# Query blocks in the order 0, 1, 3, 2: attention's projections added to totals on chip in a fused attention and product-key-expert kernel

## The chip, the cores and the metric

The kernel runs on one core of one Trainium2 chip. The metric is the device time of one execution in microseconds; the figure of a kernel is the median of its runs. The engines are called here as in the profile: PE is TensorE (matrix products), PEld its weight loads, DVE is VectorE, ACT is ScalarE, POOL is GpSimd, and SP is SyncE, which here only issues DMA transfers.

## The reference

The input is x of 2048 tokens by 512 numbers, float32. It is normalised (xn), and two parts are added to it: attention with 32 heads that share one key head and one value head of 16 numbers, and a layer of 4096 experts of which each token picks two per head by product keys.

```python
xn = _layernorm(x)
# part A: attention, one K and V head for 32 query heads
q = (xn @ wq).reshape(B, S, 32, 16).transpose(0, 2, 1, 3); k = xn @ wk; v = xn @ wv
p = softmax(einsum("bhqd,bkd->bhqk", q, k) * 16 ** -0.5)
A = einsum("bhqk,bkd->bhqd", p, v).transpose(0, 2, 1, 3).reshape(B, S, 512) @ wo
# part B: experts, 32 heads, 64 x 64 keys, two experts a head
s1, s2 = scores of the two halves of xn @ w_q against k1 and k2       # 64 each
two best of s1 and of s2 -> four candidates -> the two best (top_e), g = softmax(top_s)
act = gelu(einsum("nd,nhkd->nhk", xn, u[top_e]))
B = einsum("nhk,nhk,nhkd->nd", g, act, v[top_e])
return x + A + B
```

## The kernel before

The 2048 tokens are 16 tiles of 128 tokens, in four blocks of four tiles: block 0 is tiles 0 to 3, block 3 tiles 12 to 15. Everything is computed in one program whose instruction order is written out by hand.

**Attention.** A unit is four heads of one query block (`units`, L293); there are 32, in the order of the blocks, eight units a block. A unit goes over 16 chunks of 128 keys. For each chunk `scores` (L314) makes two score tiles on PE (L318) and their exponentials on ACT (L321), and `pv` (L324) multiplies by the values on PE (L332). Two units are a pair; `unit_tail`, `pair_load`, `pair_invert`, `pair_spread` and `pair_tail` bring the sums of the exponentials to memory and back, invert them, and write the normalised result of the pair to a tile `on`. Four pairs make a query block. Its four tiles are then multiplied by `wo`: `block_out(qb, j)` (L423) is one projection, eight matmuls of 128 x 512 into one PSUM tile (tag `x`, three buffers, which all other products share).

**Experts, by gather.** For blocks 0 and 1 each chosen expert's rows of u and v are gathered by GpSimd (L883) into one of twelve buffers (tag `g`, `NGB`), DVE takes the dot product with xn (L895), and adds the weighted row to the token's total `ACC[t]` (L930). The total starts as x, in a tile `xa` that holds total and xn of a tile of tokens. Block 1 takes over the four `xa` tiles of block 0 when that is done (`load_phase2_tile`, L988).

**Experts, dense.** For blocks 2 and 3 all 4096 experts are computed as matrix products (`dense`, L648). First a table of gates is formed by one-hot products (L752), written to memory (`d_g`, L760) and read back by blocks of experts (`fetch_gates`, L669). `first_gates` (L731) reads the first two gate blocks and loads x into the totals (`da`) of the block of tokens. Then 32 blocks of expert weights follow: `fetch` loads block b (`rw`, two buffers), `split` rounds it on ACT (L687) and takes the rest on DVE (L688), L799 multiplies by xn, ACT and DVE form the weighted activations (L821 to L835), and `sums` (L773) multiplies by v (L783) and adds to the totals (L786). The rounding of weight block b + 2 is put on the list for ACT when the product of weight block b starts (b even) or has ended (b odd).

**The order.** The outer loop runs over d; one pass is one call of `att_steps` (L1040) with i = 2d, called a step in this document: two chunks of one unit. Within a step stand, in this order: stores left by the step before (`run(STORES)`), scores of the first chunk, the products with the values of the step before, `mid()` (ACT's and DVE's lists: the copies `ON_ACT`, the dots, the expert sums, and interleaved with them the list `BEHIND`), scores of the second chunk, a projection if one is due, and `fill()`. `fill` runs the generator of the experts' scores and dense products (`run_scores`) until a count of planned work, `spent`, has reached the step's aim, which grows by (948 - 17) / 256 units a step, but by no more than 4 units in a step. A projection is booked with 3.6 units. `yield None` in the generator ends a step's fill. Two of the twelve gather buffers are lent (`lent`) to `wo` at the end of each query block.

**Where the two parts meet.** The attention part of a block and the expert part of the same block are ready at different times. `fin` is one small buffer of 128 x 512 in the pool `late`. For a projection whose experts' part isn't done (blocks 0 and 1), ACT copies the projection to `fin` (L440), and it goes to memory (`d_part`, L441); when the experts are done `experts_out` loads it into `fin` (L420), DVE adds the total (L452), and the sum is stored to `out`. For block 2 it is the other way round: the dense total goes to `d_part` first (L459), and at each projection `load_fin` brings it back, DVE adds the projection (L433), and the sum is stored. Block 3's projection and its dense total end together: `last_out_a` and `last_out_b` add the projection to `ACC[12 + j]` on chip (L411). A block's projections are due at (i - 144) % 128 = 0, 4, 8 and 12: one in every second step, in steps 144 to 156, 272 to 284 and 400 to 412.

SP issues its transfers strictly in the order of the program; one that must wait for a buffer or for data holds all that follow.

Of the kernel before, what the change touches and what calls it, by code (L numbers as in the profile page):

```python
# [11 lines left out]
F32 = mybir.dt.float32  # L12
# [11 lines left out]
P = 128  # L24
S = 2048
D = 512
# [4 lines left out]
GT = 4  # L31
# [15 lines left out]
LIMIT2 = 25000.0  # L47
C_IN = 0.7978845608028654
C_CUB = 0.044715 * C_IN
MOST = 4.0  # L50
UNIT = 0.235

# [2 lines left out]
def tile_kernel(ctx, tc, x, wq, wkv, wo, wqT, kT, uv, ub, vb, out):  # L55
    nc = tc.nc
# [4 lines left out]
    late = [None]  # L61
# [18 lines left out]
    d_part = [dram.tile([P, D], F32, name=f"dpart{t}") for t in range(NT)]  # L80
# [38 lines left out]
    gtile = lambda dt=F32, shape=(P, 1024), name="g": big.tile(list(shape), dt, name=name, tag="g", bufs=NGB)  # L119
# [4 lines left out]
    XT, XN, ACC, XP = {}, {}, {}, [None]  # L124
# [210 lines left out]
    OT, ON, RB = {}, {}, {}  # L335

    def unit_tail(u):
        pp, half = divmod(u, 2)
        e = late[0].tile([P, 512], F32, name="e", tag="e", bufs=1)
        nc.scalar.copy(e, PV.pop(u))  # L340

        def spread():
            if half == 0:
                ot = late[0].tile([P, 512], F32, name="ot", tag="ot", bufs=1)
                OT[pp] = ot
                if pp == 15:
                    rs = late[0].tile([P, 512], F32, name="rsb", tag="on", bufs=4)
                    RB[pp] = rs
            if pp < 15:
                nc.sync.dma_start(d_sum[pp, 4 * half:4 * half + 4, :],  # L350
                                  e.rearrange("(j r) n -> j r n", r=32)[:, 16, :])
            for j in range(4):
                o = slice(64 * half + 16 * j, 64 * half + 16 * j + 16)
                if pp == 15:
                    nc.sync.dma_start(RB[pp][o, :], e[32 * j + 16:32 * j + 32, :])
                (nc.scalar if u == 31 else nc.sync).dma_start(OT[pp][o, :], e[32 * j:32 * j + 16, :])

        store(spread)
# [25 lines left out]
    DONE_A, DONE_B, OUTS = {}, {}, []  # L384
    WO, lent = [], [0]

    def load_wo():
# [14 lines left out]
    def last_out_b():  # L402
        rs, ot = RB.pop(15), OT.pop(15)
        for j in range(4):
            c = slice(j * P, (j + 1) * P)
            nc.vector.reciprocal(rs[:, c], rs[:, c])
            nc.vector.tensor_mul(ot[:, c], ot[:, c], rs[:, c])
            nc.tensor.matmul(PL[j], ot[:, c], WO[1][:, 1, :], start=False, stop=True)
        for j in range(4):
            t = 12 + j  # L410
            nc.vector.tensor_add(ACC[t], ACC[t], PL[j])  # L411
            (nc.sync, nc.scalar)[j % 2].dma_start(out[t * P:(t + 1) * P, :], ACC[t])

    PL = []

    FIN = {}

    def load_fin(t):
        fin = late[0].tile([P, D], F32, name="fin", tag="fin", bufs=1)
        nc.sync.dma_start(fin, d_part[t])  # L420
        FIN[t] = fin

    def block_out(qb, j):  # L423
        t = 4 * qb + j
        p = xtile("pwo")
        for k in range(KC):
            nc.tensor.matmul(p, ON[4 * qb + k][:, j * P:(j + 1) * P], WO[k // 2][:, k % 2, :],  # L427
                             start=k == 0, stop=k == KC - 1)
        if t in FIN:
            fin = FIN.pop(t)  # L430

            def total():
                nc.vector.tensor_add(fin, fin, p)  # L433
                store(lambda: nc.sync.dma_start(out[t * P:(t + 1) * P, :], fin))

            behind(total)
        else:
            def keep():
                fin = late[0].tile([P, D], F32, name="fin", tag="fin", bufs=1)
                nc.scalar.copy(fin, p)  # L440
                store(lambda: nc.sync.dma_start(d_part[t], fin))  # L441

            on_act(keep)
        DONE_A[t] = True

    def experts_out(t):

        if t >= 12:
            return True
        if t in FIN:  # L450
            fin = FIN.pop(t)
            nc.vector.tensor_add(fin, fin, ACC[t])  # L452
            store(lambda: nc.sync.dma_start(out[t * P:(t + 1) * P, :], fin))
        elif t in DONE_A:
            load_fin(t)
            return False
        else:
            acc = ACC[t]
            store(lambda: nc.sync.dma_start(d_part[t], acc))  # L459
        DONE_B[t] = True  # L460
        return True


    WC = {}
# [183 lines left out]
    def dense(DG, after):  # L648
# [82 lines left out]
        def first_gates():  # L731

            fetch_gates(0)
            fetch_gates(1)
            for j in range(2):
                da = big.tile([P, 2, D], F32, name="da", tag="da", bufs=2)
                for i in range(2):
                    t = GT * DG + 2 * j + i
                    nc.sync.dma_start(da[:, i, :], x[t * P:(t + 1) * P, :])
                    ACC[t] = da[:, i, :]  # L740

        onehot(0)
        onehot(1)
        for q in range(NQ):
# [5 lines left out]
            p = xtile("pg")  # L750
# [40 lines left out]
        for b in range(NB):  # L791
# [3 lines left out]
            p = xtile("pact")  # L795
# [192 lines left out]
    def load_phase2_tile(t):  # L988
        xa = big.tile([P, 2, D], F32, name="xa", tag="xa", bufs=TPH)
        nc.sync.dma_start(xa[:, 1, :], d_xn[t - TPH])  # L990
        nc.sync.dma_start(xa[:, 0, :], x[t * P:(t + 1) * P, :])
        ACC[t], XN[t] = xa[:, 0, :], xa[:, 1, :]

    def load_phase2_xt(g, k):
        if k == 0:
# [41 lines left out]
    STEPS = 512  # L1037


    def att_steps(d, mid, fill):  # L1040
        i = 2 * d
        run(STORES)
        out_now = 144 <= i < STEPS and (i - 144) % 128 < 16 and i % 4 == 0
        qb, j = (i - 144) // 128, (i - 144) % 128 // 4
        if out_now and 4 * qb + j in DONE_B:
            load_fin(4 * qb + j)
        if i < STEPS:
            u, kc = divmod(i, 16)
            if i == 0:
# [97 lines left out]
    with tc.manual_schedule(engines={E_.PE, E_.Activation, E_.DVE, E_.Pool, E_.SP}):  # L1147
# [3 lines left out]
        for d in range(half + 24):  # L1151
# [9 lines left out]
            def mid():  # L1161
# [100 lines left out]
```

## Time and profile before

| | |
|---|---|
| median of three runs | 1995.04 us (1994.63 to 2007.21) |
| the profiled execution's own time | 2001.03 us |
| its span, from first to last instruction | 1999.3 us |
| PE busy | 1882.9 us (94%) |
| DVE busy | 1682.7 us (84%) |
| ACT busy | 1292.0 us (65%) |
| moved by DMA | 494.79 MB, mean 247 GB/s |
| mean granted clock of PE | 0.967 |

The profile is of one execution. Its groups of instructions give a count, the time that the engine was busy, the mean of one and the engine's idle time before them with what ended it. The view of the waits names who stood idle until whom (total, times, longest), the chain of work follows the last instruction back to what released it, and windows give each engine's busy time in a stretch of the span. Stretches are in microseconds from the span's start.

### The profile page before, as it was taken

To read this page: it belongs to the slowest core of one execution; us is meant where nothing else is said; L and a number is where in the kernel's file an instruction comes from. 1 tells how busy PE (TensorE), PEld (TensorE's weight loads), DVE (VectorE), ACT (ScalarE), POOL (GpSimd) and SP (SyncE) were. 2 spreads that over 40 slices of the span, in tenths; PEclk is the share of its full clock that TensorE was granted. 3 is DMA by queue.
4 is the path that set the end of the run, shared out by engine and by line. 5 is a ranking of instruction groups with operands and counts; after the bars stand their busy time and mean duration, and the time that the engine had idled before them with its cause. 6 is when DMAs were issued, how large, how long until landed. Compare 5 with 4: busy or idle time off the path is not lost.

```text
span 1999.3 us, 34729 instructions
## 1 busy us (share of the span) xinstructions
PE 1882.9 (94%) x10990; PEld 997.5 (50%) x10990; DVE 1682.7 (84%) x6713; ACT 1292.0 (65%) x1804; POOL 570.8 (29%) x542
## 2 busy tenths in 40 slices
PE   6869999999998998999999999999899789999997
PEld 4534444555554444555555455555445345555552
DVE  7537888999998786999999779999999668999993
ACT  3236666655556785787877565555568567788873
POOL 2202232222222232333444222222223333333320
PEclk9989999999997998999999999999979899999999
DMA  7847878977664878888889877777568877888762
GB/s 272 301 185 235 276 272 272 331 275 248 218 212 140 229 221 271 264 269 269 284 297 328 286 253 261 268 238 225 176 169 234 276 245 263 268 277 257 263 211 63
DMA packets 239882, 494.79 MB, mean 247 GB/s; under 512 B 93380, under 2 KB 93380, under 8 KB 239692
## 3 DMA queue, kind: packets, MB, share of 16 engines
q0 software_dynamic: 73728, 268.47, 40.5%
q1 hardware_dynamic: 163960, 222.44, 34.0%
q10 hardware_dynamic: 2004, 1.61, 0.3%
q8 instruction: 88, 1.44, 0.3%
q14 instruction: 102, 0.84, 0.1%
HBM read 429.51 MB, written 57.64 MB: 244 GB/s over the span
## 4 chain that ended last, share of the span: by engine, by line
PE 63%; DVE 20%; DMA 5%; issue 2%; ACT 2%; SPq 1%; DVEq 0%; ACTq 0%
PE pv L332 18%; PE sc L318 12%; PE psc L532 10%; PE pout L783 8%; PE pact L799 8%; DVE i L547 5%; DVE xa L930 4%; DVE m L545 3%; DVE g L895 3%; PE pg L752 3%; PE pw L487 2%; PE pwo L427 1%; DMA dg<-gst 1%; ACT pt L321 1%; DMA fin<-dpart 1%
## 5 line engine op out<-in xcount | busy, mean ns | idle before, releaser
L321 ACT ACTIVATE pt<-sc 128x1024 f32<-128x1024 f32 x1024 | 993.0, 1025 | 471.1 <-PE sc L318 424.6
L883 POOL DMA_INDIRECT g<-in_uv_dram,idx x512 | 554.0, 1082 | 1358.4 <-DVE xa L930 697.4
L332 PE MATMUL pv<-pt,vaug 128*32 128x512 f32 x4096 | 524.1, 631 | 0.0
L318 PE MATMUL sc<-qa,kaug 64*128 64x512 f32 x2048 | 389.1, 454 | 14.4 <-ACT pt L321 13.5
L532 PE MATMUL psc<-wk,xt 128*128 128x512 f32 x1536 | 388.2, 400 | 5.3 <-DMA xt<-dxt 3.2
L930 DVE SCALAR_TENSOR_TENSOR xa<-g,w,xa 128x512 f32<-128x512 f32 x512 | 370.6, 745 | 0.0
L895 DVE CUSTOM_DVE_ANT_0 g<-g,xa 128x512 f32<-128x512 f32 x512 | 336.1, 681 | 3.0 <-DMA g<-in_uv_dram,idx 3.0
L532 PEld LDWEIGHTS psc<-wk,xt 128*128 128x128 f32 x1536 | 277.8, 188 | 108.7 <-issue 38.5
L318 PEld LDWEIGHTS sc<-qa,kaug 64*128 64x128 f32 x2048 | 157.6, 187 | 338.2 <-ACT pt L321 203.5
L332 PEld LDWEIGHTS pv<-pt,vaug 128*32 128x32 f32 x4096 | 110.7, 113 | 263.4 <-issue 261.7
L799 PE MATMUL pact<-xt,wk 128*128 128x512 f32 x768 | 198.7, 404 | 14.6 <-DVE fin L433 6.3
L547 DVE FIND_INDEX8 i<-m,psc 128x8 uint32<-128x64 f32 x1024 | 206.4, 221 | 0.0
L783 PE MATMUL pout<-wk,wd 128*128 128x512 f32 x768 | 195.7, 402 | 8.7 <-DVE wd L835 4.7
L799 PEld LDWEIGHTS pact<-xt,wk 128*128 128x128 f32 x768 | 141.1, 190 | 65.4 <-issue 17.7
L783 PEld LDWEIGHTS pout<-wk,wd 128*128 128x128 f32 x768 | 140.6, 188 | 56.7 <-DVE wd L835 6.0
L545 DVE MAX8 m<-psc 128x8 f32<-128x64 f32 x1024 | 146.0, 214 | 22.2 <-PE psc L532 19.8
L786 DVE TENSOR_TENSOR da<-da,pout 128x512 f32<-128x512 f32 x128 | 82.7, 679 | 8.2 <-PE pout L783 7.9
L918 DVE SCALAR_TENSOR_TENSOR w<-gth,ga 128x4 f32<-128x4 f32 x128 | 20.2, 158 | 79.9 <-ACT gth L911 79.4
L688 DVE TENSOR_TENSOR wk<-rw,wk 128x512 fp32r<-128x512 f32 x128 | 84.8, 682 | 0.1
L725 DVE TENSOR_TENSOR oh<-oh 128x2048 f16<-128x2048 f16 x64 | 78.0, 1219 | 7.1 <-PE pg L752 7.1
L752 PE MATMUL pg<-oh 128*128 128x32 f16 x1024 | 73.4, 246 | 8.1 <-DVE oh L728 8.1
L687 ACT CAST wk<-rw 128x512 fp32r<-128x512 f32 x128 | 73.6, 628 | 9.0 <-DMA rw<-in_ub_dram 6.7
(150 smaller groups left out, 1341.8 us busy)
## 6 DMA issues: line engine op xcount, KB each, us to landing
wk<-dw SPq DMA_DIRECT2D x96, 512.0 KB
wqt<-in_wqT_dram SPq DMA_DIRECT2D x32, 512.0 KB
dw<-wk SPq DMA_DIRECT2D x32, 512.0 KB
rw<-in_ub_dram SPq DMA_DIRECT2D x64, 256.0 KB
rw<-in_vb_dram SPq DMA_DIRECT2D x64, 256.0 KB
dg<-gst SPq DMA_DIRECT2D x32, 512.0 KB
gy<-dg SPq DMA_DIRECT2D x64, 256.0 KB
qa<-dqh SPq DMA_DIRECT2D x128, 64.0 KB
```

The source lines that it names most:

```text
L318: nc.tensor.matmul(p[:, b, :], kaug[o:o + 64, kc * P:(kc + 1) * P], QA[u][o:o + 64, i, :], start=True, stop=True)
L321: nc.scalar.activation(pt, p, AF.Exp, scale=SCALE)
L332: nc.tensor.matmul(PV[u][32 * j:32 * j + 32, :], vaug[:, kc, :], pt[:, b, :], start=kc == 0, stop=kc == 15)
L532: nc.tensor.matmul(p, XT[g][k][:, a, j * P:(j + 1) * P], WC[n_][k][:, bb, :], start=n == 0, stop=n == 11)
L545: nc.vector.max(m8[:, jb, s, :], p[:, s * E:(s + 1) * E])
L547: nc.vector.max_index(i8[:, jb, s, :], m8[:, jb, s, :], p[:, s * E:(s + 1) * E])
L752: nc.tensor.matmul(p[:, i * NB:(i + 1) * NB], oa[:, :, i], ob[:, :, i], start=True, stop=True)
L783: nc.tensor.matmul(p, wd[:, a, j * P:(j + 1) * P], vs[:, c, :], start=n == 0, stop=n == 5)
L799: nc.tensor.matmul(p, us[:, a, k * P:(k + 1) * P], XT[DG][k][:, c, :], start=n == 0, stop=n == 11)
L883: nc.gpsimd.indirect_dma_start(out=gt, out_offset=None, in_=uv, in_offset=bass.IndirectOffsetOnAxis(ap=IDX[ph, c, ti][:, s:s + 1], axis=0))
L895: nc.vector.tensor_tensor_reduce(u, u, XN[TPH * ph + ti], scale=1.0, scalar=0.0, op0=OP.mult, op1=OP.add, accum_out=a[:, i:i + 1])
L930: nc.vector.scalar_tensor_tensor(acc, v, w[:, i:i + 1], acc, op0=OP.mult, op1=OP.add)
```

## The change

The order of the query blocks becomes 0, 1, 3, 2 (`QB`). Attention's third block is then block 3, whose dense totals are being formed on chip at that time, and its last block is block 2, whose dense totals are finished long before. So a projection of the first three blocks is added by DVE straight to the total on chip (`ACC[t]`), before the experts' last term or between them; nothing of attention goes to `d_part`, and `fin` is gone. Of the dense totals, only those of block 2 go to `d_part`; they come back once, near the end, into two of the gather buffers (`load_last`), and `last_out_b` adds the last projections there. Finished totals of the other blocks go to `out` as they are, one a step.

A finished query block puts its four projections on a list (`PWO`) at i % 128 = 16. For block 1 they are emitted as before, one in every second step. For blocks 0 and 3 they are held until i % 128 = 28 (`HOLD`) and are then emitted one a step: steps 156 to 162 and 412 to 418. The lent buffers go back 6 later there (i % 128 = 36). The tag `on` has five buffers for four.

```diff
+HOLD = 28
...
-    units = [(qb, hg) for qb in range(4) for hg in range(8)]
+    QB = (0, 1, 3, 2)
+    units = [(qb, hg) for qb in QB for hg in range(8)]
...
-        on = late[0].tile([P, 512], F32, name="on", tag="on", bufs=4)
+        on = late[0].tile([P, 512], F32, name="on", tag="on", bufs=5)
...
         for j in range(4):
-            t = 12 + j
-            nc.vector.tensor_add(ACC[t], ACC[t], PL[j])
-            (nc.sync, nc.scalar)[j % 2].dma_start(out[t * P:(t + 1) * P, :], ACC[t])
+            t = GT * QB[3] + j
+            nc.vector.tensor_add(FT[t], FT[t], PL[j])
+            (nc.sync, nc.scalar)[j % 2].dma_start(out[t * P:(t + 1) * P, :], FT[t])
...
-    def load_fin(t):
-        fin = late[0].tile([P, D], F32, name="fin", tag="fin", bufs=1)
-        nc.sync.dma_start(fin, d_part[t])
-        FIN[t] = fin
...
-    def block_out(qb, j):
-        t = 4 * qb + j
+    LIVE = set(range(GT))
+    PWO = []
+
+    def block_out():
+
+        m, j = PWO.pop(0)
+        t = GT * QB[m] + j
         p = xtile("pwo")
         for k in range(KC):
-            nc.tensor.matmul(p, ON[4 * qb + k][:, j * P:(j + 1) * P], WO[k // 2][:, k % 2, :],
+            nc.tensor.matmul(p, ON[4 * m + k][:, j * P:(j + 1) * P], WO[k // 2][:, k % 2, :],
                              start=k == 0, stop=k == KC - 1)
-        if t in FIN:
...
-            behind(total)
-        else:
-            def keep():
...
-            on_act(keep)
+        assert t in LIVE
+        acc = ACC[t]
+        behind(lambda: nc.vector.tensor_add(acc, acc, p))
         DONE_A[t] = True
 
+    def out_ready():
+        return PWO and GT * QB[PWO[0][0]] + PWO[0][1] in LIVE
+
     def experts_out(t):
...
+        acc, last = ACC[t], t // GT == QB[3]
+        assert last or t in DONE_A
+        store(lambda: nc.sync.dma_start(d_part[t] if last else out[t * P:(t + 1) * P, :], acc))
+        LIVE.discard(t)
+
+    FT = {}
+
+    def load_last():
+        for i in range(2):
+            w = gtile(F32, (P, 2, D), "ft")
+            for j in range(2):
+                t = GT * QB[3] + 2 * i + j
+                nc.sync.dma_start(w[:, j, :], d_part[t])
+                FT[t] = w[:, j, :]
...
-        out_now = 144 <= i < STEPS and (i - 144) % 128 < 16 and i % 4 == 0
-        qb, j = (i - 144) // 128, (i - 144) % 128 // 4
-        if out_now and 4 * qb + j in DONE_B:
-            load_fin(4 * qb + j)
+        if 144 <= i < STEPS and i % 128 == 16:
+            PWO.extend((i // 128 - 1, j) for j in range(4))
...
-        if out_now:
-            block_out(qb, j)
+        if out_ready() and (i % 128 >= HOLD and PWO[0][0] != 1 or i % 4 == 0 and PWO[0][0] == 1):
+            block_out()
             spent[0] += 3.6
         fill()
...
+        if i == STEPS - 6:
+            load_last()
-        if i >= 128 and i % 128 == 30:
+        if i >= 128 and i % 128 == (30 if 256 < i < 384 else HOLD + 8):
             lent[0] = 0
...
-                    if OUTS and (2 * d < 140 or (2 * d - 140) % 128 >= 24) and experts_out(OUTS[0]):
-                        OUTS.pop(0)
+                    if OUTS:
+                        experts_out(OUTS.pop(0))
```

`LIVE` holds the tiles whose totals are on chip: tiles 0 to 3 from the start, others from the load of their totals (`first_gates`, `load_phase2_tile`).

More of the change, by code (lines that the diff above doesn't have):

```diff
@@ L346, in spread @@
                 if pp == 15:
-                    rs = late[0].tile([P, 512], F32, name="rsb", tag="on", bufs=4)
+                    rs = late[0].tile([P, 512], F32, name="rsb", tag="on", bufs=5)
                     RB[pp] = rs
@@ L379, in pair_tail @@
         rs = RB.pop(pp)
-        on = late[0].tile([P, 512], F32, name="on", tag="on", bufs=4)
+        on = late[0].tile([P, 512], F32, name="on", tag="on", bufs=5)
         nc.vector.tensor_mul(on, OT.pop(pp), rs)
         ON[pp] = on
-    DONE_A, DONE_B, OUTS = {}, {}, []
+    DONE_A, OUTS = {}, []
     WO, lent = [], [0]
@@ L423, in block_out @@
-    def block_out(qb, j):
-        t = 4 * qb + j
+    LIVE = set(range(GT))
[3 more added lines that the diff above has]
+        t = GT * QB[m] + j
         p = xtile("pwo")
         for k in range(KC):
-            nc.tensor.matmul(p, ON[4 * qb + k][:, j * P:(j + 1) * P], WO[k // 2][:, k % 2, :],
+            nc.tensor.matmul(p, ON[4 * m + k][:, j * P:(j + 1) * P], WO[k // 2][:, k % 2, :],
                              start=k == 0, stop=k == KC - 1)
-        if t in FIN:
[L430 to L434, printed above, removed]
-            behind(total)
-        else:
-            def keep():
-                fin = late[0].tile([P, D], F32, name="fin", tag="fin", bufs=1)
-                nc.scalar.copy(fin, p)
-                store(lambda: nc.sync.dma_start(d_part[t], fin))
-            on_act(keep)
+        assert t in LIVE
+        acc = ACC[t]
+        behind(lambda: nc.vector.tensor_add(acc, acc, p))
@@ L444, in block_out @@
         DONE_A[t] = True
+    def out_ready():
+        return PWO and GT * QB[PWO[0][0]] + PWO[0][1] in LIVE
     def experts_out(t):
[L448 to L459, printed above, removed]
@@ L460, in experts_out @@
-        DONE_B[t] = True
-        return True
+        acc, last = ACC[t], t // GT == QB[3]
[10 more added lines that the diff above has]
+                FT[t] = w[:, j, :]
@@ L740, in first_gates @@
                     ACC[t] = da[:, i, :]
+                    LIVE.add(t)
         onehot(0)
@@ L992, in load_phase2_tile @@
         ACC[t], XN[t] = xa[:, 0, :], xa[:, 1, :]
+        LIVE.add(t)
     def load_phase2_xt(g, k):
```

1 line of the change is left out of this document (removed).

## The prediction

> **What bounds the kernel now.** I read the page first, then the windows of single stages, then waits, chain and timeline of the stages in which TensorE is not full.
>
> ```profile
> span 1999.3 us, 34729 instructions
> PE 1882.9 (94%) x10990; PEld 997.5 (50%) x10990; DVE 1682.7 (84%) x6713; ACT 1292.0 (65%) x1804; POOL 570.8 (29%) x542
> PE 63%; DVE 20%; DMA 5%; issue 2%; ACT 2%; SPq 1%; DVEq 0%; ACTq 0%
> ```
>
> TensorE (PE) sets the pace: 94% busy and 63% of the chain that ended last. The change does the same matrix work in another order, so it can only pay where PE stands. To find those places I counted the exponentials L321, four to a step of attention (a step is one call of `att_steps`, i = 0, 2, ... 510, two chunks of keys), and cut the trace at steps. The gates of the dense experts of block 2 are ready in step 172 (748.7 us), those of block 3 in step 400 (1565.2 us). Here are the five steps from there and the next five, for each block (length; busy us of PE, PEld, DVE, ACT and POOL, with instructions; granted clock; DMA share; GB/s):
>
> ```profile
> 748.70:799.10 50.40, 40.60 (x200) 20.54 (x200) 32.58 (x75) 29.95 (x44) 13.18 (x14) 0.86 0.82 275
> 799.10:836.80 37.70, 37.70 (x212) 21.60 (x210) 36.19 (x85) 29.51 (x44) 14.32 (x13) 1.00 0.76 245
> 1565.20:1615.60 50.40, 39.80 (x177) 16.81 (x175) 26.07 (x64) 25.79 (x37) 14.24 (x15) 0.86 0.84 276
> 1615.60:1656.30 40.70, 36.96 (x193) 18.49 (x193) 31.77 (x73) 27.35 (x39) 17.13 (x14) 0.96 0.76 265
> ```
>
> Five undisturbed steps take 37.7 us. Both starts of the dense experts take 50.4, with PE idle 9.8 and 10.6 us. Only the second has projections and the loads into `fin` in it, so the reader should see that equal length hides two different causes. These are the waits of 1560 to 1660 us:
>
> ```profile
> DVE fin L433 <- DMA fin<-dpart: 25.3, 3, 12.9
> ACT gy L842 <- DVE gy L822: 13.8, 1, 13.8
> PE pact L799 <- DVE fin L433: 6.3, 1, 6.3
> PE pout L783 <- DVE fin L433: 3.6, 1, 3.6
> ```
>
> VectorE stands 25.3 us, in three waits, for a total on its way back into the one `fin` buffer, and what queues behind its add (the sums L930, the splits L688, the polynomial L822) holds up ScalarE and PE; PE's direct share is 9.9 us. At the first start it is another wait (740 to 800 us):
>
> ```profile
> ACT wk L687 <- DMA rw<-in_ub_dram: 6.7, 1, 6.7
> PE pact L799 <- ACT wk L687: 5.0, 1, 5.0
> ```
>
> ScalarE stands at L687, the rounding of the fourth block of expert weights (block 3, `rw`), which is loaded too late; behind it wait the exponentials.
>
> **Part 1: block 3's projections leave steps 400 to 412, and the `fin` wait goes.** The chain of waits at both starts, and SP's queue at the second:
>
> ```profile
> 745.58 14.97 DMA dg<-gst
> 763.78 11.24 DMA rw<-in_vb_dram
> 1568.58 13.71 DMA dg<-gst
> 1585.77 5.20 DMA fin<-dpart
> ```
>
> ```profile
> 1582.35 0.81 SPq L675 DMA_DIRECT2D gy<-dg  x2
> 1583.20 2.52 SPq L739 DMA_DIRECT2D da<-in_x_dram  x4
> 1585.77 0.43 SPq L420 DMA_DIRECT2D fin<-dpart  x1
> 1586.30 0.56 SPq L350 DMA_DIRECT2D dsum<-e  x1
> 1586.90 2.44 SPq L356 DMA_DIRECT2D ot<-e  x4
> 1589.43 0.53 SPq L657 DMA_DIRECT2D rw<-in_ub_dram  x1
> 1590.01 0.43 SPq L658 DMA_DIRECT2D rw<-in_vb_dram  x1
> ```
>
> SP sits until the gates are written (13.71 us), then issues gates, totals, `fin`, the unit's rows, and only then weight block 3. Taking `fin` out saves this queue 0.5 us. Who needs weight block 3, and when? Its rounding is put into the step after the product of weight block 1. The planner gives a step (948 - 17) / 256 = 3.6 units and books 3.6 for a projection. Before, the projections in steps 400 and 404 leave block 0's product (2.8 units, after which the step ends) to be finished in 402 and block 1's in 406; the rounding comes in step 408, where nothing waits:
>
> ```profile
> 1612.20 1.14 ACT L687 CAST wk<-rw 128x512 fp32r<-128x512 f32 x2
> 773.10 0.62 ACT L687 CAST wk<-rw 128x512 fp32r<-128x512 f32 x1 [6.67 <-DMA rw<-in_ub_dram]
> ```
>
> Without them steps 400 and 402 hold the products of blocks 0 and 1, as 172 and 174 did, and the rounding comes in step 404, about 1581 us, as it came in 176 at the first start. So **the projections were also the cover of a late load**, and this is what is late next: ScalarE now stops at L687 in place of L842. The release: the second half is issued at 1590.01 - 0.5 = 1589.5. Its landing is bounded by 5.20 us (the `fin` load, issued 3.7 us earlier behind the same six loads) and 11.24 (the same load at the first start, straight behind the same six loads, with the next weight block right after it). I take 7, nearer to the first, since the unit's small rows now part it from the six: 1596.5, with 1594.7 and 1600.7 as ends. At the first start it landed at 775.0, 26.3 us after the window's start; now it is 31.3 (29.5 to 35.5), 5.0 us later (3.2 to 9.2). The first five steps take 50.4 + 5.0 = 55.4 us (53.6 to 59.6), where they took 50.4.
>
> On landing the Trainium skill has a rule (DMA: Bandwidth & Descriptors, Anatomy of one DMA): a fixed 2 us plus the bytes over 436 GB/s. By that estimate 256 KB would land after 2.6 us and the sum below would be 4.4 us less; the rows here say 5.20 and 11.24, with the DMA engines 84% busy, so the trace does not bear it out in this stage.
>
> The next five steps now hold all four projections, one a step in 412 to 418, with one step of dense work ahead. One step's attention and one projection:
>
> ```profile
> 1581.10 0.73 PE L318 MATMUL sc<-qa,kaug 64*128 64x512 f32 x4
> 1579.25 1.92 PE L332 MATMUL pv<-pt,vaug 128*32 128x512 f32 x16
> 1581.76 3.70 PE L427 MATMUL pwo<-wo,on 128*128 128x512 f32 x8
> 1596.50 1.71 PE L318 MATMUL sc<-qa,kaug 64*128 64x512 f32 x4 [1.77 <-ACT pt L321]
> ```
>
> That is 2 x 0.73 + 1.92 + 3.70 = 7.1 us; four of them and one plain step (37.7 / 5 = 7.5) make 35.9, against 40.7 (bounds 34, five steps of the 6.8 us that a full step mostly takes, and 38). A projection is booked alike in both, so at step 420 the same dense work is done, to a fraction of a budget unit. Ten steps: 55.4 + 35.9 = 91.3, against 91.1: **+0.2 us** (53.6 + 34 - 91.1 = -3.5; 59.6 + 38 - 91.1 = +6.5). Below that, if the late load held up nothing at all, ten steps would take 75.4: -15.7.
>
> The last row above shows PE after a stand: four score matmuls take 1.71 us, not 0.73. The windows of both starts have a granted clock of 0.86. The Trainium skill has it as a rule that speaks against the change (TensorE: Matmul & The Clock Gate, What's actually happening): one idle window of some 3.4 us and the array runs at half rate until it has been busy for another. The row agrees that PE starts slow. By the rule two stands over 3.4 us (6.3 and 3.6) that become one save one such start, an estimate of 3.4 / 2 = 1.7 us off the sum.
>
> **Part 2: block 0's projections move from steps 144 to 156 (every second) to 156 to 162.** Both lie in the stage in which gates are formed, where PE is full (620 to 740 us in three windows, summed):
>
> ```profile
> sum 120.00, PE 119.77 PEld 59.38 DVE 94.24 ACT 91.79 POOL 28.44; mean PE 39.92 PEld 19.79 DVE 31.41 ACT 30.60 POOL 9.48
> ```
>
> The same 32 matmuls and the same gate products; I put 0 (-2 to +3).
>
> **Part 3: eight copies by ScalarE become adds by VectorE.**
>
> ```profile
> L440 ACT COPY fin<-pwo 128x512 f32<-128x512 f32 x8 | 4.8, 595 | 0.3 <-DMA dpart<-fin 0.3
> L452 DVE TENSOR_TENSOR fin<-fin,xa 128x512 f32<-128x512 f32 x8 | 5.5, 684 | 5.3 <-DMA fin<-dpart 5.3
> L532 PEld LDWEIGHTS psc<-wk,xt 128*128 128x128 f32 x1536 | 277.8, 188 | 108.7 <-issue 38.5 <-DVE i L547 4.8 <-DMA xt<-dxt 4.1
> ```
>
> ScalarE, 65% busy, loses 4.8 us that PE covers. VectorE gains eight adds at the projections and loses the eight of L452: 0. But the projection's PSUM buffer, one of three, is now freed in VectorE's order, behind a step's products and searches. That can bite in steps 272 to 284, where scores of experts need these buffers. PE's weight loads have waited 4.8 us for VectorE there in the whole run; bounds 0 and another 4.8, and I take +0.5, since four adds stand against 1024 searches.
>
> **Part 4: traffic.** Gone are eight stores and eight loads of 256 KB (4.2 of 494.8 MB). In the chain, and in the waits after it, a load of sums takes long among stores and loads of totals:
>
> ```profile
> 1083.20 9.82 DMA rc<-dsum
> DVE rc L370 <- DMA rc<-dsum: 2.6, 1, 2.6
> ```
>
> VectorE waits 2.6 us for it. I take -0.5 (-3 to 0).
>
> **Part 5: the tail.** Block 2's dense totals come back into two large buffers in step 506. VectorE idles 14.6 us before its last reciprocals, which covers that. But tiles 12 to 15 are now stored one a step behind the last experts, and SP runs in order:
>
> ```profile
> 1985.00 0.95 DVE L406 RECIPROCAL rsb<-rsb 128x128 f32<-128x128 f32 x1 [14.63 <-DMA rsb<-e]
> 1990.47 1.53 SPq L412 DMA_DIRECT2D out_dram<-da  x2
> 1992.10 0.96 SPq L392 DMA_DIRECT2D wo<-in_wo_dram  x2
> GB/s 0 0 0 0 0 0 0 0 0 0 0 102 112 118 84 0 0 0 0 0 0 0 6 0 30 104 207 63 0 0 0 83 370 222 302 407 228 0 0 0
> ```
>
> The stores of tiles 14 and 15 come after the L412 pair, which waits for the last sums. The last row is what moved in slices of 1950 to 1999.3 us: some 300 GB/s at the end, so 0.5 MB more cost 1.7 us; I take +1.5 (0 to 3.5).
>
> **Sum:** 0.2 + 0 + 0.5 - 0.5 + 1.5 = +1.7 us on the span of 1999.3. The profiled execution's own time is 2001.0, 6 above the median of the runs, 1995.0; the same difference on the median gives **1996.7 us**. One per cent, about what a measurement of this kernel can tell from no change, is 20 us.
>
> **The rivals.**
> *The wait goes and nothing takes its place.* For it: 25.3 us of VectorE's waits stand on `fin`, and L842 no longer waits 13.8. Against it: the first start has no `fin` and is just as long. It needs weight block 3 to land before ScalarE asks, about 1581, eight us before it is issued; or PE to have enough other work. In full it gives -15.7 + 1.5 = -14.2: 1981.
> *The late load costs more than `fin` did* (the other side). If the second half lands later than 1597 (11.24 us as at the first start, or more, with the gathers no longer held back by VectorE), ScalarE stands 19 us, PE cools, and weight blocks 4 and 5 come late too: +6.5 in part 1, and with the upper ends of parts 3 and 5 (4.8 and 3.5) about +15: 2010.
> *Four steps of projections alone empty the dense pipeline.* No product of weights runs in 412 to 418, so the next sums find nothing formed, and the restart costs what step 178 cost (10.4 against 7.5) once or twice: +1.7 + 5 = 2002. Against it: activations already begun flow on during these steps.
> *It doesn't do what it says:* totals of block 2 still leave the chip and come back once. That changes neither sum, as the tail covers it.
>
> **How the numbers follow.** The forecast, with -3.5 to +6.5 about it, 0.55; no replacement wait 0.17; the late load dearer 0.18; the emptied pipeline 0.10. The range reaches from the first rival to the second, 1981 to 2011. Faster by over 1% needs the whole first rival and more: 0.07. Slower by over 1% needs the second with something on top of it: 0.10. Within 1%: 0.83.
>
> **What would show it.** Right: no row waits for `fin`; L687 waits 10 to 19 us for `rw` near 1581; the ten steps from 1565 take 88 to 98 us; one projection each in steps 412 to 418 at about 7.1 us; two `out` stores on SP after the last pair. Wrong: L687 near 1581 waits less than 5 us, ten steps under 85 us, or steps 272 to 284 longer than 6.8 us each by more than 1 us.

## The result, and the profile after

| | before | after | ratio, 95% interval |
|---|---|---|---|
| first comparison, 20 runs each | 1995.36 us | 2004.6 us | 1.0044 (1.0025 to 1.0062) |
| again, 35 and 13 runs | 1998.89 us | 2003.24 us | 1.0028 (1.0002 to 1.0053) |
| the profiled execution's own time | 2001.03 us | 1994.84 us | |

The change makes the kernel slower by 0.3 to 0.4%, well within 1%. The two profiled executions point the other way, because executions of one kernel spread over some 20 us (1989.24 to 2007.21 before, 1993.31 to 2014.38 after). So two whole traces can't be compared here; single stages of several traces can. The page of after:

```profile
span 1993.0 us, 34680 instructions
PE 1875.5 (94%) x10990; PEld 1001.5 (50%) x10990; DVE 1683.1 (84%) x6713; ACT 1287.8 (65%) x1796; POOL 565.7 (28%) x542
PE 60%; DVE 24%; DMA 4%; ACT 2%; issue 2%; SPq 0%; ACTq 0%; DVEq 0%
```

The matrix work is the same 10990 products, and ACT has the eight copies less. (Line numbers have shifted: the rounding of weights is now L678, its subtraction L679, the product with xn L791, the loads of gates L666, of x L730, of weights L648 and L649, the store of the gates L752, the projection's add L432, VectorE's product with the gates L817; in `cover_back`, `cover_again` and `x_early_held` the later lines stand two or four further down.) The waits of 1550 to 1650 us, where block 3's dense experts start:

```profile
ACT wk L678 <- DMA rw<-in_ub_dram: 14.8, 1, 14.8
PE pact L791 <- ACT wk L678: 11.8, 1, 11.8
DVE gy L817 <- DMA gy<-dg: 7.3, 1, 7.3
```

No row names a total on its way back. In its place ScalarE stands 14.8 us for weight block 3, and PE 11.8 us behind it. VectorE stands 7.3 us for the first gates at the same time; that wait ends first, at 1581.2 us. What came before that in SP's queue, the stand on ACT, and the three longest transfers in the chain of waits:

```profile
1559.47 9.04 SPq L752 DMA_DIRECT2D dg<-gst  x2
1572.88 0.81 SPq L666 DMA_DIRECT2D gy<-dg  x2
1573.74 2.33 SPq L730 DMA_DIRECT2D da<-in_x_dram  x4
1576.11 0.55 SPq L353 DMA_DIRECT2D dsum<-e  x1
1578.66 3.67 SPq L359 DMA_DIRECT2D ot<-e  x4
1582.54 0.41 SPq L648 DMA_DIRECT2D rw<-in_ub_dram  x1
1583.20 1.56 SPq L649 DMA_DIRECT2D rw<-in_vb_dram  x1
...
1586.07 0.62 ACT L678 CAST wk<-rw 128x512 fp32r<-128x512 f32 x1 [14.79 <-DMA rw<-in_ub_dram]
...
1559.47 13.39 DMA dg<-gst
...
1574.79 8.39 DMA da<-in_x_dram
...
1583.20 3.86 DMA rw<-in_vb_dram
```

ScalarE asked at 1586.07 - 14.79 = 1571.3 us, before SP had even been released by the store of the gates (1559.47 + 13.39 = 1572.9). The windows of the first five and the next five steps from step 400, after, and before in a second trace (`before_b`):

```profile
1555.80:1613.90 58.10, 40.47 (x200) 21.62 (x198) 36.71 (x83) 30.97 (x46) 17.16 (x16) 0.82 0.77 259
1613.90:1648.70 34.80, 34.80 (x172) 14.14 (x170) 25.45 (x64) 24.34 (x32) 13.01 (x13) 1.00 0.71 226
...
1567.50:1617.30 49.80, 38.72 (x177) 16.52 (x175) 26.35 (x67) 25.81 (x36) 14.58 (x15) 0.90 0.85 277
1617.30:1656.30 39.00, 35.41 (x193) 18.14 (x193) 31.91 (x73) 27.48 (x39) 17.17 (x14) 1.00 0.81 285
```

After loses 8 us in the first five steps (PE idle 17.6 of 58.1 us) and gets 4 to 6 back in the next five, in which PE is busy throughout. Ten steps: 92.9 against 88.8 and the 91.1 of the first trace.

### The profile page after: what moved, and what is told of

The parts are those of the page before. It is cut to its first block, busy times and chain, and to the rows that moved or that the text cites. A ratio compares the mean times of both kernels' runs of the same rounds, so it can differ in the third digit from the quotient of the medians.

```text
span 1993.0 us, 34680 instructions
## 1 busy us (share of the span) xinstructions
PE 1875.5 (94%) x10990; PEld 1001.5 (50%) x10990; DVE 1683.1 (84%) x6713; ACT 1287.8 (65%) x1796; POOL 565.7 (28%) x542
## 3 DMA queue, kind: packets, MB, share of 16 engines
q1 hardware_dynamic: 161656, 218.24, 33.6%
## 4 chain that ended last, share of the span: by engine, by line
PE 60%; DVE 24%; DMA 4%; ACT 2%; issue 2%; SPq 0%; ACTq 0%; DVEq 0%
PE pv L335 16%; PE sc L321 12%; PE psc L523 10%; PE pout L775 8%; PE pact L791 8%; DVE i L538 5%; DVE xa L922 4%; DVE g L887 3%; DVE m L536 3%; PE pwo L428 2%; DVE oh L716 2%; PE pw L478 2%; ACT pt L324 1%; PE pg L744 1%; DMA rw<-in_vb_dram 1%
## 5 line engine op out<-in xcount | busy, mean ns | idle before, releaser
L335 PE MATMUL pv<-pt,vaug 128*32 128x512 f32 x4096 | 509.4, 615 | 0.0
L775 PE MATMUL pout<-wk,wd 128*128 128x512 f32 x768 | 201.0, 411 | 10.8 <-DVE wd L827 10.5
L791 PE MATMUL pact<-xt,wk 128*128 128x512 f32 x768 | 196.7, 402 | 14.7 <-ACT wk L678 11.8
L775 PEld LDWEIGHTS pout<-wk,wd 128*128 128x128 f32 x768 | 144.5, 193 | 59.5 <-DVE wd L827 12.2
L791 PEld LDWEIGHTS pact<-xt,wk 128*128 128x128 f32 x768 | 140.4, 189 | 64.6 <-issue 19.0
L679 DVE TENSOR_TENSOR wk<-rw,wk 128x512 fp32r<-128x512 f32 x128 | 85.0, 685 | 0.0
L678 ACT CAST wk<-rw 128x512 fp32r<-128x512 f32 x128 | 73.5, 628 | 15.6 <-DMA rw<-in_ub_dram 14.8
```

The costliest lines, as they stand in the source:

```text
L335: nc.tensor.matmul(PV[u][32 * j:32 * j + 32, :], vaug[:, kc, :], pt[:, b, :], start=kc == 0, stop=kc == 15)
L775: nc.tensor.matmul(p, wd[:, a, j * P:(j + 1) * P], vs[:, c, :], start=n == 0, stop=n == 5)
L791: nc.tensor.matmul(p, us[:, a, k * P:(k + 1) * P], XT[DG][k][:, c, :], start=n == 0, stop=n == 11)
```

## The experiments

Stages are compared by steps, found from the exponentials as in the prediction. "Ten steps" are 400 to 420, the tail is from step 508 to the end. Theory A: block 3's projections were the cover of a late load of weight block 3; whoever moves them away trades the wait for the totals for a wait for weights.

**The two kernels once more.** `after_again` is after, unedited.

> The changed kernel once more, for its spread and a second trace on the chip of the runs beside it. Theory A (the late weight block): the changed kernel loses where the rounding of weight block 3 waits for its load in step 404 (14.8 us of ScalarE's time in the trace so far); in this trace the ten steps 400 to 420 take 88 to 100 us against 91.1 in the trace of before. Theory B (elsewhere): those ten steps are no longer than before's and the loss is in steps 128 to 180, in 264 to 272 or behind step 508. Time 1.000 to 1.008 of before.

It gave the second line of the table, and ten steps of 90.9 us with ScalarE standing 13.4 us for the weights. `before_b` is before, unedited.

> The kernel before, traced a second time, without an edit: it tells which stretches of the two traces compared differ by more than two executions of one kernel do. Theory A (the change costs time in its own stretches: steps 144 to 172 about 3.5 us, steps 264 to 272 one to three us, steps 400 to 420 one us, the tail 1.3 us): steps 144 to 172 again at 85 to 87 us, 264 to 272 at 29 to 30.5, 400 to 420 at 90 to 92, the tail at 35.5 to 36. Theory B (these stretches wander by themselves as 128 to 144 and 172 to 182 do): one or more of them lies over 3 us from the first trace, 144 to 172 at 88 to 91 among them.

Ten steps took 88.8 us, the tail 36.2, steps 264 to 272 31.8 and steps 144 to 172 87.4. `before_noload` (below) gives a third trace of these stages: 87.0, -, 32.7, 88.9. (The dash: that kernel's tail is another one.) `before_b` alone fits neither expectation: all four stages lie outside the ranges of theory A, and none lies over 3 us from the first trace, as theory B asked. With the third trace the first one (91.1, 35.7, 29.7, 85.3) is at an end of its own kernel's spread in three stages, and 3 to 4 us from the other end.

**Move the projections without the totals.** `before_held2` is the kernel before, with block 2's projections in 412 to 424; the totals still leave the chip and come back. A third line of the edit, not printed here, holds the store of finished totals 12 steps longer as well; it was held up to step 420 before, so nothing of that falls into the ten steps.

```diff
-        out_now = 144 <= i < STEPS and (i - 144) % 128 < 16 and i % 4 == 0
-        qb, j = (i - 144) // 128, (i - 144) % 128 // 4
+        late2 = 12 if i >= 400 else 0
+        out_now = 144 <= i < STEPS and 0 <= (i - 144) % 128 - late2 < 16 and i % 4 == 0
+        qb, j = (i - 144) // 128, ((i - 144) % 128 - late2) // 4
...
-        if i >= 128 and i % 128 == 30:
+        if i >= 128 and i % 128 == (42 if 400 <= i < 512 else 30):
```

> The kernel before with one edit: the projections of query block 2 stand in steps 412, 416, 420 and 424 instead of 400 to 412; the totals still leave the chip and come back for block 3's dense part as before. Theory A of the prediction (the projections were also the cover of a late load of weight block 3): a ScalarE wait of 10 to 15 us for that load appears in step 404 although nothing else has changed, steps 400 to 406 take 35 to 37 us against 32.2, and the wait for the totals that come back gets shorter by part of that. Its rival (the wait for the totals alone sets these steps): no wait for the weights over 3 us, and steps 400 to 420 grow by what the later store of the totals adds, 10 us or more (101 to 105 us against 91.1). By theory A the sum of steps 400 to 420 is 91 to 98 us, since the moved projections then lie beside steps that have no other gap.

Its waits of 1550 to 1650 us and its two windows:

```profile
ACT wk L687 <- DMA rw<-in_ub_dram: 15.8, 2, 15.1
PE pact L799 <- ACT wk L687: 12.0, 1, 12.0
...
1555.40:1611.30 55.90, 39.28 (x200) 20.24 (x198) 36.33 (x83) 31.04 (x46) 17.19 (x16) 0.85 0.81 268
1611.30:1646.10 34.80, 34.80 (x186) 16.74 (x184) 29.01 (x69) 25.38 (x34) 11.22 (x11) 1.00 0.76 250
```

This shows theory A: with the projections moved and nothing else changed in the ten steps, after's wait for the weights is there (15.1 us), no row names a wait for a total, and ten steps take 90.7 us, not the 101 or more of its rival.

**Leave the projections where they were.** `unhold3` is after, with block 3's projections back in steps 400 to 412.

```diff
-        if out_ready() and (i % 128 >= HOLD and PWO[0][0] != 1 or i % 4 == 0 and PWO[0][0] == 1):
+        if out_ready() and (i % 128 >= HOLD and PWO[0][0] == 0 or i % 4 == 0 and PWO[0][0] != 0):
...
-        if i >= 128 and i % 128 == (30 if 256 < i < 384 else HOLD + 8):
+        if i >= 128 and i % 128 == (30 if 256 < i else HOLD + 8):
```

> The changed kernel with block 3's projections back where they were, one in every second step from step 400 (and the lent buffers back at 30); totals stay on chip, no small buffer. Theory A (the projections were the cover of the late load): the product of weight block 1 is again finished in step 406, its rounding follows in 408, and no row waits for weight block 3; VectorE now waits for the load of x into the total of tile 12 in step 402 (5 to 10 us, once) where it waited for the small buffer three times (25 us); ten steps 400 to 420 take 80 to 86 us, the time is 6 to 14 us below the changed kernel and up to 8 below before. Theory B: no gain over the changed kernel (within 3 us).

1996.42 us, 0.9985 (0.9955 to 1.0014) of before and 6.8 us under `after_again`. Its waits of 1560 to 1650 us and its windows:

```profile
DVE da L432 <- DMA da<-in_x_dram: 9.9, 1, 9.9
PE pact L791 <- DVE da L432: 3.1, 1, 3.1
...
1564.60:1609.30 44.70, 38.59 (x179) 16.63 (x177) 31.07 (x76) 25.65 (x36) 16.96 (x17) 0.92 0.97 310
1609.30:1644.20 34.90, 34.90 (x193) 18.03 (x191) 27.75 (x64) 27.35 (x39) 12.33 (x12) 1.00 0.74 255
```

Ten steps take 79.6 us, 12 less than after and 9 less than before. The time of the whole kernel is only 2.5 us under before's, with an interval from 9 us less to 3 more, so what the stage gains is not shown for the whole. No row of these waits names the first half of weight block 3 (`in_ub`), and the wait for the gates is down to 2.7 us. One longer wait is left: the first projection is added to a total whose x is still being loaded, 9.9 us.

**Load the weights ahead of the gates.** `gates_late` is after, with `first_gates` issued one step later, behind weight block 3.

```diff
-                        store(first_gates)
+                        store(lambda: AFTER.append(first_gates))
...
+        held = AFTER[:]
+        AFTER.clear()
         run(STORES)
+        run(held)
```

> The changed kernel with the first two gate loads and the load of x into the dense totals issued one step later, behind the load of weight block 3; nothing else. Theory A: weight block 3 is issued some 5 us (first start) to 11 us (second start) earlier, so ScalarE's wait at its rounding near step 404 falls from 14.8 us to 4 to 9, the ten steps 400 to 420 fall from 92.9 to 82 to 88, and the time is 5 to 15 us below the changed kernel. Theory B: ScalarE's wait falls, but another (the gates, now later) takes its place, and the time stays within 3 us.

2001.86 us, 1.0002 (0.9972 to 1.0031) of before. The waits of 1572 to 1668 us:

```profile
DVE gy L817 <- DMA gy<-dg: 13.0, 3, 9.3
ACT wk L678 <- DMA rw<-in_ub_dram: 9.3, 2, 8.4
PE pact L791 <- DVE gy L897: 7.6, 1, 7.6
```

Ten steps take 87.5 us: 3 to 5 less than after's 90.9 and 92.9. The wait for weights shrank to 8.4 us, and gates that now come late hold VectorE for 9.3 us (7.3 in after); PE, which stood for ScalarE's weights in after, now stands 7.6 us for VectorE. The stage is as theory A expected it; the time is not (1.4 us under `after_again`, where A said 5 to 15) and is as theory B had it. In this one queue both transfers are late for the held order, and putting one first makes PE wait for the other.

**Cover, and x loaded early.** `cover_back` is after with the projections of every block in every second step from i % 128 = 16, the x of the totals loaded from within the gate loop, all finished totals stored at once, and without a last load of `wo` that nothing reads.

```diff
         def first_gates():
...
             fetch_gates(1)
+
+        def first_totals():
             for j in range(2):
                 da = big.tile([P, 2, D], F32, name="da", tag="da", bufs=2)
...
+                    if t0 == 320:
+                        store(first_totals)
                     if t0 == 448:
                         store(first_gates)
...
-        if out_ready() and (i % 128 >= HOLD and PWO[0][0] != 1 or i % 4 == 0 and PWO[0][0] == 1):
+        if out_ready() and i % 4 == 0:
...
-        if i >= 128 and i % 128 == 10 or i == STEPS - 10:
+        if 128 <= i < STEPS and i % 128 == 10 or i == STEPS - 10:
...
-        if i >= 128 and i % 128 == (30 if 256 < i < 384 else HOLD + 8):
+        if i >= 128 and i % 128 == 30:
...
-                    if OUTS:
+                    while OUTS:
                         experts_out(OUTS.pop(0))
```

> The kernel after with the order of blocks and the additions on chip kept, but every block's projections again in every fourth step from its first gap on (so 144 to 156, 272 to 284, 400 to 412), the dense totals' x loaded early, from within the gate loop, so that the first addition has no load to wait for, and the end drained as in tail_drained. Theory A (the wait for the totals can go only where the projections stay as cover for the load of weight block 3): no ScalarE wait for the weights over 3 us in steps 400 to 406, no VectorE wait for x near 10 us, steps 400 to 420 at 72 to 78 us against 92.9, steps 144 to 172 at 85 to 87 against 88 to 91, tail at 36 or less; ratio 0.990 to 0.995. Rival (the time of these steps is given back by what follows, or the gates' loads then end last): steps 400 to 420 at 79 us or more, or 420 to 508 longer by the same amount; ratio 0.997 to 1.001.

1975.96 us, 0.9883 (0.9851 to 0.9915) of before: faster than both kernels. The gain is above the range of theory A, and so is that of the ten steps (71.4 us; expected 72 to 78); steps 144 to 172 took 88.8 us, not 85 to 87. `cover_again` is the same kernel beside `before_noload`.

> cover_back once more, beside before_noload on one chip. Theory A: the gain lies in steps 400 to 420 (71 to 73 us against 88 to 92) and in the tail (32.3), nothing elsewhere; ratio to before 0.987 to 0.991, and to before_noload 0.989 to 0.993. Rival (its first result owed several us to steps that wander from one execution to the next): ratio to before above 0.992.

1975.08 us, 0.9865 (0.9838 to 0.9892) of before, and 1975.08 / 2000.78 = 0.987 of `before_noload`; both ratios lie just below their expected ranges. Its ten steps, SP's queue and the rounding of weight block 3 on ScalarE:

```profile
1562.20:1597.10 34.90, 34.90 (x179) 15.50 (x177) 28.04 (x68) 25.60 (x36) 16.42 (x15) 1.00 0.99 324
1597.10:1631.90 34.80, 34.80 (x193) 18.04 (x191) 29.20 (x68) 27.27 (x38) 14.86 (x14) 1.00 0.84 296
...
1564.70 9.29 SPq L754 DMA_DIRECT2D dg<-gst  x2
1583.91 0.33 SPq L648 DMA_DIRECT2D rw<-in_ub_dram  x1
1585.23 0.34 SPq L649 DMA_DIRECT2D rw<-in_vb_dram  x1
...
1590.76 1.13 ACT L678 CAST wk<-rw 128x512 fp32r<-128x512 f32 x2
```

PE is busy for all of 69.7 us, and at full clock. Weight block 3 is issued 4.4 us earlier than in after: its second half 1585.23 - 1562.2 = 23.0 us after step 400 began, against 27.4. That alone would not do, since in after ScalarE asked 1571.3 - 1555.8 = 15.5 us after step 400 began. Here it asks only in step 408, 1590.76 - 1562.2 = 28.6 us after, with projections in between, and waits for nothing. This is the cover that the prediction spoke of, now without a wait for totals.

`x_early_held` is `cover_back` with the hold of after put back, so with x early and projections late (block 0's as well, which lie outside these steps).

```diff
-        if out_ready() and i % 4 == 0:
+        if out_ready() and (i % 128 >= HOLD and PWO[0][0] != 1 or i % 4 == 0 and PWO[0][0] == 1):
...
-        if i >= 128 and i % 128 == 30:
+        if i >= 128 and i % 128 == (30 if 256 < i < 384 else HOLD + 8):
```

> cover_back with the projections of the first and the last block held again as in the kernel after (block 3's in steps 412 to 418), so that of cover_back's edits to steps 400 to 420 only the early load of x is left. Together with after, unhold3 and cover_back it makes the four cases of held or not held with x late or early; the three measured so far in steps 400 to 420: held and late 93.0, 90.8 and 92.8 us, not held and late 79.6, not held and early 71.4. Theory A (the cover sets these steps; the early load helps only where the first addition would wait for it): the ScalarE wait for weight block 3 stays at 10 to 13 us, steps 400 to 420 take 88 to 92 us. Rival (the 1 MB of x ahead of the weights in SP's queue is what makes them late): wait under 7 us, steps 400 to 420 at 84 us or less.

The waits of 1555 to 1655 us:

```profile
ACT wk L678 <- DMA rw<-in_ub_dram: 10.4, 1, 10.4
DVE gy L821 <- DMA gy<-dg: 8.8, 2, 8.0
```

Ten steps took 86.0 us, between the two expectations. So the four cases in ten steps are:

| | x late | x early |
|---|---|---|
| projections held | 92.9, 90.9, 92.8, 90.8, 92.2 | 86.0 |
| not held | 79.6 | 71.4, 69.7 |

The hold costs 12 to 16 us, x behind the gates 6 to 9. The first is the larger share. Theory A expected that x has nothing to do with the held case; the one trace, below all five beside it, speaks against that.

**Block 0's projections.** `early0` is after, with block 0's projections back in steps 144 to 156.

```diff
-        if out_ready() and (i % 128 >= HOLD and PWO[0][0] != 1 or i % 4 == 0 and PWO[0][0] == 1):
+        if out_ready() and (i % 128 >= HOLD and PWO[0][0] == 2 or i % 4 == 0 and PWO[0][0] != 2):
...
-        if i >= 128 and i % 128 == (30 if 256 < i < 384 else HOLD + 8):
+        if i >= 128 and i % 128 == (30 if i < 384 else HOLD + 8):
```

> The changed kernel with block 0's projections back in steps 144 to 156, one in every second step. Theory A: no difference to the changed kernel (within 3 us), since PE is full in that stage and the same work is done. Theory B: the place of block 0's projections is part of the loss, 3 to 9 us are won back, and steps 156 to 180 show it.

1998.1 us, 1.0005 (0.9975 to 1.0034) of before. Over all traces, steps 144 to 172 take 84.2 to 93.5 us with the projections held (seven traces, mean 88.4) and 85.3 to 92.3 not held (seven, mean 88.2). The traces show no cost; the median is 5 us below `after_again` beside it, with intervals that overlap. Whether this part costs anything stays open.

**The end.** Three kernels: `tail_drained` is after with the last two edits of `cover_back`; `after_noload` and `before_noload` leave out the last load of `wo` alone, which nothing reads.

> The kernel after with two edits to its end: all finished totals are stored at once and not one per pair, and the second load of the projections' weights, which nothing reads, is not issued. Theory A (the 1.3 us that the tail grew by is the two stores that now stand behind the last pair): the tail goes from 37.0 to 35.7 us or less. Rival (the tail is set by the chain of the last experts, and the stores lie beside it): 36.8 to 37.2 us. All other stretches as after.

> The kernel after without the second load of the projections' weights (512 KB) that it issues last and nothing reads; totals are still stored one per pair, so two of them behind the last pair. If two stores and load each add their part (1.3 and 3.4 us, as the tails of before, after and tail_drained go: 35.7, 37.0, 32.3), the tail is 33.3 to 33.9 us. If the load alone made the end, 32.2 to 32.6; if the stores did, 36 or more.

> The kernel before without the same load, which it issues last too. Theory (the end waits for that load's landing): tail 32.0 to 33.0 us against 35.7 and 36.2, steps 400 to 420 as before at 88 to 92; ratio 0.9975 to 0.999. It gives the kernel that cover_back has to be compared with when the change itself is judged, since this edit has nothing to do with it.

What SP issues last in after, in `after_noload` and in `tail_drained`, in this order:

```profile
1982.80 1.53 SPq L415 DMA_DIRECT2D out_dram<-ft  x2
1984.37 0.95 SPq L441 DMA_DIRECT2D out_dram<-da  x2
1985.43 1.82 SPq L395 DMA_DIRECT2D wo<-in_wo_dram  x2
...
1988.50 1.53 SPq L415 DMA_DIRECT2D out_dram<-ft  x2
1990.08 0.97 SPq L441 DMA_DIRECT2D out_dram<-da  x2
...
1985.47 1.53 SPq L415 DMA_DIRECT2D out_dram<-ft  x2
```

The tails are 37.0, 33.6 and 32.3 us; before has 35.7 and 36.2, without the load 33.6. So in after the load (two transfers of 512 KB, 1 MB together, not the 512 KB of the expectation) costs 3.4 us and the two late stores 1.3 (33.6 - 32.3), as the sum of parts had it. In before the load costs 2.1 to 2.6, less than I expected, and its removal can't be told from no change in the time: 2000.78 us, 0.9992 (0.9969 to 1.0016).

## Why the prediction was right, and where it was off

The forecast was no change within 1%, with the wait for `fin` replaced by a wait for weight block 3. That is what happened, and `before_held2` and `unhold3` show it from both sides: the late load is there as soon as the projections move, and gone when they stay.

**Part 1, the first five steps: the moment was right by two errors.** Weight block 3 landed 1583.20 + 3.86 - 1555.8 = 31.3 us after the window's start, the figure forecast. But it was issued at 27.4, not 24.3: SP stood 2.0 us between the rows of `dsum` and `ot`, which the view of SP's own waits puts down to the store of the gates, and those four loads took 3.67 us where I had read 2.44. And it landed after 3.86 us, not 7, below the lower bound of 5.20, while a load of x of the same size ahead of it took 8.39 (in the chain, its landing stands just before the issue of this second half). That the two errors cancelled is luck. (ScalarE began on the first half, 1.0 us before the second landed.) The Trainium skill's rule (DMA: Bandwidth & Descriptors, Anatomy of one DMA: 2 us plus bytes over 436 GB/s, an estimate of 2.6 us) was nearer to this landing than the 7 us that I took; the page gives it for transfers that GpSimd issues, and these are issued by SP, which my prediction did not say. The sum that I worked out by it was nonetheless further from the trace, since the issue was late.

The five steps took 58.1, 2.7 more than the 55.4 forecast, inside its bounds of 53.6 and 59.6. Beside the wait for the weights another wait of PE had grown, by 1.8 us: it stood 3.2 us for VectorE's weighted activations (L775 on L827 in after), and 1.4 at the first start. The next five took 34.8 against 35.9, and steps 412 to 418 6.8 us each, not 7.1. Ten steps: 91.3 forecast, 90.8 to 92.9 in five traces with the hold and x late, mean 91.9.

**What failed most is what this was set against.** I took 91.1 us from the one trace; two more traces of before gave 88.8 and 87.0, mean of three 89.0. So part 1 costs about 2.9 us, not 0.2; the three and the five traces just touch in their ranges. In the same way the median of three runs, 1995.0, was low: with more runs beside them the same kernel had 1995.4, 1998.9, 1998.6 and 2001.2. The absolute forecast of 1996.7 is 7.9 us under the result, of which the difference forecast (1.7 against 4.4 to 9.2) is a part.

**The rule on the clock gate.** By the Trainium skill (TensorE: Matmul & The Clock Gate, What's actually happening) fewer long stands should have saved 1.7 us, by my estimate. There was no saving to see: the first five steps had a granted clock of 0.82 in after, below the 0.86 and 0.90 of before, as one long stand took the place of two shorter ones. In the traces shown, the granted clock of these steps goes with PE's idle time in them: 1.00 with none (`cover_again`), 0.92 with 6.1 us (`unhold3`), 0.86 and 0.90 with 10.6 and 11.1 (before), 0.85 with 16.6 (`before_held2`), 0.82 with 17.6 (after). So an idle PE goes with a lower clock in this stage, as the rule has it; the count of stands, on which my estimate rested, does not tell by how much.

**Parts 2 to 4.** No cost of part 2 in the traces (0 forecast). Steps 272 to 284 stayed at 6.8 us, so the 0.5 for the adds on VectorE was not spent. The gain of 0.5 in part 4 is not to be seen: steps 264 to 272 took 29.7 to 32.7 us in before and 30.4 to 33.6 in after and its relatives. The means, 31.1 of four traces and 32.6 of ten, would rather allow for a cost of 1.5 us there, inside the spread.

**Part 5.** +1.3 us between the first traces (37.0 against 35.7), forecast +1.5. What I missed stood in the row that I had quoted: the load of `wo` costs 3.4 us of the tail, more than the two late stores, and nothing reads it.

What is located, 2.9 us in ten steps and about 1 us in the tail, makes 3.9 of the 4.4 to 9.2 us. The rest, up to 5 us, is not located. The traces may not hold it: the two traced executions of after took 1994.84 and 1985.99 us, 10 and 17 under the medians beside them.

**Where the gain of the change went.** Taking the totals off the path alone is worth 89.0 - 79.6 = 9 us in ten steps, and 18 to 19 together with x in time. (An early x was not tried in the kernel before, so what it would bring there is open.) Holding the projections back spends all of the 9, by letting loads be late that the projections used to cover: weight block 3 first, and the first gates beside it. `cover_back` against before gains 22.7 us by the medians: 89.0 - 71.4 = 17.6 in ten steps and 36.0 - 32.3 = 3.7 in the tail.

## What to carry to other kernels

Work that stands between a request and its need is a cover, even if it was put there for another reason; before moving it, ask which load becomes the last one. When two edits come together, measure each alone: here one gained 9 us or more and the other spent it, and the sum looked like nothing. And a term of two or three microseconds needs more than one trace of the kernel before.

## What the runs showed of the hardware

The spread between executions goes with the granted clock of TensorE. Over 63 executions of before whose clock is listed, it ranged from 0.957 to 0.973, and a straight line through them gives 1.8 us more for each 0.001 less (correlation -0.81); over 33 of after 1.6 us (-0.85). The twelve of `cover_back` stay within 0.968 to 0.974 and 1971.27 to 1980.3 us.

A clock below one was also granted where PE was not idle. Steps 368 to 384, in which one-hot products form the gates, in `early0` and in after:

```profile
1456.10:1510.60 54.50, 54.50 (x450) 26.90 (x448) 48.34 (x96) 40.42 (x68) 13.99 (x12) 0.79 0.72 192
...
1457.40:1505.00 47.60, 45.63 (x450) 25.95 (x448) 44.16 (x89) 40.18 (x69) 14.26 (x12) 0.97 0.77 200
```

The same 450 matmuls take 54.5 us with PE busy throughout, at a clock of 0.79, and 47.6 us at 0.97. What lowers it there was not tried and stays open.
